# Weight conversion in a Strassen-style matmul kernel: three DVE passes put side by side, and GpSimd's addition made one instruction

## The chip, the cores and the metric

The kernel runs on one core of one Trainium2 chip. The metric is the device time of one execution in microseconds (us), lower is better. Each kernel was run several times, on the same chip in turn with the kernel before. Engines: PE is TensorE, DVE is VectorE, ACT is ScalarE, POOL is GpSimd.

## The reference

A cross attention between `x` and `state` gives 4352 rows of 512 numbers; they go through two weight matrices with a cosine gate between:

```python
h = x @ w_in              # (4352, 512) @ (512, 2048)
g = h * np.cos(h)
return (g @ w_out).astype(np.float32)
```

The matrices come as float64 (`randn(...).astype(float32)` times a NumPy float64 scalar), and the kernel turns both into float32 itself, from the raw 32-bit words.

## The kernel before

The program is one list of instructions for each engine, written in steps; a step makes one 128x512 tile of `h`, gates it, and lets TensorE multiply the gated tile of three steps ago with `w_out`. Steps 0 to 15 (about 30 to 130 us) also convert the weights, one load of 128x1024 elements a step. A load passes through three engines:

```python
if p == "1":   nc.scalar.activation(dst, raw_high_word, func=ACTF.Abs)
elif p == "2": nc.scalar.activation(e, raw_low_word, func=ACTF.Copy, scale=2.0 ** -51, bias=2.0)
elif p == "a": nc.vector.tensor_scalar(dst, dst, 2.0 ** -15, None, op0=ALU.max)          # limit
elif p == "b": nc.vector.tensor_scalar(bits, bits, 3, None, op0=ALU.logical_shift_left)  # shift
elif p == "c": nc.vector.scalar_tensor_tensor(out=bits, in0=raw_high, scalar=-2 ** 31, in1=bits,
                                              op0=ALU.bitwise_and, op1=ALU.bitwise_xor)  # sign
else:                                                                                    # d, the sum
    n = 1 if i < 4 else 2
    for j in range(n):
        r = slice(m * j // n, m * j // n + m // n)
        nc.gpsimd.tensor_tensor(bits[:, r], bits[:, r], e.bitcast(I32)[:, r], op=ALU.add)
```

(The views of the raw words are shortened here.) The loop over steps, cut to what matters:

```python
hidden(t)                          # PE: the tile h
go(0)                              # PE: attention and column-block products of this step
gate(t); gate2(t)                  # ACT: round; DVE: distance
go(1); go(3)                       # ACT and DVE: copies, attention
if last >= 0: convert(last, "cd")  # DVE c, POOL d of the load of the step before
gate3(t)                           # ACT: Abs, Sin
gate4(t)                           # DVE: gate product h * cos
...
if conv >= 0: convert(conv, "2")   # ACT, this step's load ("1" is further up)
go(4)
if conv >= 0: convert(conv, "ab")  # DVE
...                                # PE: output products of an earlier tile
```

So DVE's row in a step is gate2, c, gate4, a, b.

## Time and profile before

| | before |
|---|---|
| median of 6 runs | 821.08 us (820.25 to 821.51) |
| profiled span | 818.6 us |
| busy PE, DVE, ACT, POOL | 779.7, 435.0, 397.6, 184.0 us |
| PE idle from 30 to 135 us | 19.1 us |
| PE idle from 160 to 750 us | 4.2 us |

The busy shares of the whole run hide that there are two stages: up to about 130 us TensorE waits for the others, afterwards it is full. What is gained in the first stage moves the whole second stage forward. The lines for this are in the prediction.

### The profile page before, as it was taken

To read this page: it belongs to the slowest core of one execution; us is meant where nothing else is said; L and a number is where in the kernel's file an instruction comes from. 1 tells how busy PE (TensorE), PEld (TensorE's weight loads), DVE (VectorE), ACT (ScalarE), POOL (GpSimd) and SP (SyncE) were. 2 spreads that over 40 slices of the span, in tenths; PEclk is the share of its full clock that TensorE was granted. 3 is DMA by queue.
4 is the path that set the end of the run, shared out by engine and by line. 5 is a ranking of instruction groups with operands and counts; after the bars stand their busy time and mean duration, and the time that the engine had idled before them with its cause. 6 is when DMAs were issued, how large, how long until landed. Compare 5 with 4: busy or idle time off the path is not lost.

```text
span 818.6 us, 7603 instructions
## 1 busy us (share of the span) xinstructions
PE 779.7 (95%) x2736; PEld 349.9 (43%) x2736; DVE 435.0 (53%) x671; ACT 397.6 (49%) x644; POOL 184.0 (22%) x135
## 2 busy tenths in 40 slices
PE   6788788989999999999999999999999999999997
PEld 3233234334434443444444344444344444455554
DVE  3899897653355435863454456743554355432431
ACT  2667775554447444644455444634473445322222
POOL 2244237876100000154000000451000002620200
PEclk7899999999999999999999999999999999999999
DMA  6575350101000211030010211120000112100021
GB/s 154 180 213 178 123 155 1 26 8 45 1 15 12 52 26 26 13 65 0 1 26 7 58 23 16 33 46 0 14 14 0 27 26 54 75 1 13 14 38 38
DMA packets 111653, 37.19 MB, mean 45 GB/s; under 512 B 103616, under 2 KB 103616, under 8 KB 111616
## 3 DMA queue, kind: packets, MB, share of 16 engines
q1 hardware_dynamic: 108800, 35.93, 18.1%
q10 hardware_dynamic: 2688, 0.66, 0.4%
q8 instruction: 21, 0.34, 0.2%
q0 software_dynamic: 128, 0.13, 0.1%
q14 instruction: 16, 0.13, 0.1%
HBM read 27.79 MB, written 8.91 MB: 45 GB/s over the span
## 4 chain that ended last, share of the span: by engine, by line
PE 78%; DVE 11%; ACT 7%; issue 1%; DMA 1%; POOL 0%; ACTq 0%; DVEq 0%; POOLq 0%
PE o L504 42%; PE h L439 25%; PE at L291 4%; PE o L621 3%; DVE q L448 2%; PE at L378 2%; ACT q L454 1%; PE at L264 1%; DVE g_all L460 1%; ACT q L453 1%; DVE xT L311 1%; DVE aT L355 1%; ACT xT L337 1%; DVE w_in L226 1%; DVE w_in L221 1%
## 5 line engine op out<-in xcount | busy, mean ns | idle before, releaser
L439 PE MATMUL h<-aT,sw 128*128 128x512 f32 x512 | 247.8, 607 | 16.4 <-DVE g_all L460 11.9
L504 PE MATMUL o<-g_all,w_out 128*128 128x512 f32 x512 | 238.7, 603 | 4.5 <-DVE sw L418 2.9
L466 POOL TENSOR_TENSOR g_all<-g_all 128x512 f32<-128x512 f32 x80 | 112.0, 1421 | 460.7 <-DVE g_all L460 455.7
L445 ACT ACTIVATE q<-h 128x512 f32<-128x512 f32 (+1 forms) x144 | 82.2, 571 | 270.2 <-PE h L439 270.2
L448 DVE SCALAR_TENSOR_TENSOR q<-q,h 128x512 f32<-128x512 f32 (+1 forms) x144 | 94.2, 654 | 208.8 <-ACT q L445 208.8
L504 PE MATMUL o<-g_all,s 128*128 128x512 f32 x384 | 177.3, 598 | 0.0
L460 DVE TENSOR_TENSOR g_all<-h,q 128x512 f32<-128x512 f32 (+1 forms) x144 | 94.8, 658 | 139.5 <-ACT q L454 139.3
L439 PEld LDWEIGHTS h<-aT,sw 128*128 128x128 f32 x512 | 98.0, 194 | 145.5 <-issue 112.1
L504 PEld LDWEIGHTS o<-g_all,w_out 128*128 128x128 f32 x512 | 93.9, 190 | 127.1 <-issue 120.6
L453 ACT ACTIVATE q<-q 128x512 f32<-128x512 f32 (+1 forms) x144 | 87.5, 608 | 103.7 <-DVE q L448 103.7
L504 PEld LDWEIGHTS o<-g_all,s 128*128 128x128 f32 x384 | 70.3, 190 | 88.4 <-issue 83.6
L454 ACT ACTIVATE q<-q,halfpi 128x512 f32<-128x512 f32 (+1 forms) x144 | 100.5, 698 | 4.5
L236 POOL TENSOR_TENSOR w_out<-w_out,s 128x512 int32<-128x512 int32 x20 | 27.2, 1379 | 84.8 <-DVE w_out L226 80.0
L466 DVE TENSOR_TENSOR g_all<-g_all 128x512 f32<-128x512 f32 x48 | 33.2, 692 | 1.6
L439 PE MATMUL h<-sT,w_in 128*128 128x256 f32 x128 | 30.2, 379 | 0.0
L236 POOL TENSOR_TENSOR w_in<-w_in,s 128x512 int32<-128x512 int32 x16 | 21.7, 1369 | 37.7 <-DVE w_in L226 37.7
L420 ACT COPY sw<-at 128x512 f32<-128x512 f32 x48 | 25.7, 588 | 9.0 <-PE at L291 9.0
L621 PE MATMUL o<-w_out,g_all 128*128 128x512 f32 x64 | 29.6, 592 | 0.0
L439 PEld LDWEIGHTS h<-sT,w_in 128*128 128x128 f32 x128 | 24.3, 190 | 10.1 <-issue 6.7
L510 DVE SCALAR_TENSOR_TENSOR held<-o,held 128x512 f32<-128x512 f32 x40 | 25.4, 681 | 3.7 <-PE o L504 3.7
L291 PE MATMUL at<-w_in,stT 64*32 64x512 f32 x384 | 26.1, 601 | 0.0
L531 DVE STREAM_TRANSPOSE ot<-held 128x512 f32<-128x512 f32 x32 | 22.2, 694 | 0.0
(84 smaller groups left out, 472.5 us busy)
## 6 DMA issues: line engine op xcount, KB each, us to landing
out_dram<-ot SPq DMA_DIRECT2D x136, 64.0 KB, 2.0
g_all<-in_moe_w_out_dram SPq DMA_DIRECT2D x8, 1024.0 KB, 5.0
x_b<-in_x_dram SPq DMA_DIRECT2D x60, 128.0 KB, 2.9
g_all<-in_moe_w_in_dram SPq DMA_DIRECT2D x6, 1024.0 KB, 5.2
g_all<-in_moe_w_in_dram SPq DMA_DIRECT2D x4, 512.0 KB, 5.6
x_b<-in_moe_w_out_dram SPq DMA_DIRECT2D x1, 1024.0 KB, 5.7
xT<-in_moe_w_out_dram SPq DMA_DIRECT2D x1, 1024.0 KB, 7.8
x_b<-in_x_dram ACTq DMA_DIRECT2D x4, 128.0 KB, 4.7
```

The source lines that it names most:

```text
L236: nc.gpsimd.tensor_tensor(bits[:, r], bits[:, r], e.bitcast(I32)[:, r], op=ALU.add)
L291: nc.tensor.matmul(out=(to or at)[j][Ns * k:Ns * k + Ns, 0:n], lhsT=w[D * j:D * j + D, self.b, Ns * k:Ns * k + Ns], rhs=r(slice(D * j, D * ...
L420: nc.scalar.copy(dst, to[j][:, 0:c1 - c0])
L439: nc.tensor.matmul(out=t.hp, lhsT=t.lhs(i), rhs=t.rhs(i), start=(i == 0), stop=(i == t.kn - 1))
L445: nc.scalar.activation(t.q, t.hp, func=ACTF.Copy, bias=MAGIC)
L448: nc.vector.scalar_tensor_tensor(out=t.q, in0=t.q, scalar=MAGIC, in1=t.hp, op0=ALU.subtract, op1=ALU.subtract)
L453: nc.scalar.activation(t.q, t.q, func=ACTF.Abs)
L454: nc.scalar.activation(t.q, t.q, func=ACTF.Sin, bias=halfpi, scale=-TWO_PI)
L460: nc.vector.tensor_tensor(t.g, t.hp, t.q, op=ALU.mult)
L466: engine.tensor_tensor(out, a, b, op=ALU.subtract)
L504: nc.tensor.matmul(out=acc[bank][ch], lhsT=w[:, i, P * ch:P * ch + P], rhs=g.g, start=(i == 0), stop=(i == NH - 1))
L621: nc.tensor.matmul(out=acc[MAIN][i], lhsT=t.g[:, P * i:P * i + P], rhs=w_out[:, :, t.f, :], start=(n == 0), stop=(n == NF - 1))
```

## The change

The intent: limit and shift leave the end of a step, where GpSimd's sum of the load before is running and blocks them (limit takes 1.32 and shift 1.64 us there, 54.76 to 57.75 us, against 0.68 and 0.69 us with GpSimd idle, at 753.9 us), and stand beside the sign, in the time that ACT takes from distance to gate product. GpSimd's sum becomes one instruction in place of two halves. The whole diff (blank lines left out):

```diff
-            n = 1 if i < 4 else 2
-            for j in range(n):
-                r = slice(m * j // n, m * j // n + m // n)
-                nc.gpsimd.tensor_tensor(bits[:, r], bits[:, r],
-                                        e.bitcast(I32)[:, r], op=ALU.add)
+            nc.gpsimd.tensor_tensor(bits, bits, e.bitcast(I32), op=ALU.add)
@@ before step 0
     a0.exp2()
-    convert(3, "ab")
@@ in the step, between gate2 and gate4
         if last >= 0:
-            convert(last, "cd")
+            convert(last, "abcd")
@@ at the end of the step
         go(4)
-        if conv >= 0:
-            convert(conv, "ab")
```

## The prediction

> **What bounds the kernel now.** I read the 40 slices first, then the busy times by stretch, then the chain of waits from 30 to 130 us, and last the instructions of VectorE (DVE) and GpSimd (POOL) there in order of time.
>
> ```profile
> PE   6788788989999999999999999999999999999997
> PEld 3233234334434443444444344444344444455554
> DVE  3899897653355435863454456743554355432431
> ```
>
> One slice is 20.5 us. From the eighth slice TensorE is full to the end; only the first six (to about 130 us) leave it idle, and there DVE is at 80 to 90%. By stretch (start:end, length, then busy time and count of PE, weight loads, DVE, ACT, POOL; granted clock, DMA share, GB/s):
>
> ```profile
> 30.00:60.00 30.00, 24.24 (x112) 10.46 (x111) 25.35 (x37) 21.59 (x32) 10.87 (x9) 0.89 0.70 211
> 60.00:90.00 30.00, 26.16 (x104) 10.63 (x103) 28.43 (x36) 20.15 (x28) 13.25 (x10) 0.94 0.52 176
> 90.00:110.00 20.00, 14.65 (x61) 5.74 (x61) 16.05 (x22) 15.35 (x23) 5.44 (x4) 0.91 0.30 104
> 110.00:135.00 25.00, 20.88 (x78) 8.38 (x75) 21.28 (x28) 17.38 (x26) 13.37 (x10) 0.93 0.30 86
> 160.00:750.00 590.00, 585.77 (x2038) 259.32 (x2037) 289.05 (x460) 281.52 (x464) 107.32 (x75) 1.00 0.12 24
> ```
>
> Between 30 and 135 us TensorE's idle is 5.76 + 3.84 + 5.35 + 4.12 = 19 us of 105; from 160 to 750 us it is 4 of 590. So the change can only earn in these 105 us, and at most 19 us, 2.3% of 821. These are the sixteen first tiles (steps 0 to 15), during which the weights are turned into float32, one load a step. The chain of waits goes here through DVE and ACT. Two steps of DVE, in order of time (start, duration, line):
>
> ```profile
> 52.89 1.23 DVE L226 SCALAR_TENSOR_TENSOR w_out<-g_all,w_out 128x1024 int32<-128x1024 int32 x1
> 54.15 0.69 DVE L460 TENSOR_TENSOR g_all<-h,q 128x512 f32<-128x512 f32 x1
> 54.76 1.32 DVE L221 TENSOR_SCALAR w_in<-w_in 128x1024 f32<-128x1024 f32 x1
> 56.11 1.64 DVE L223 TENSOR_SCALAR w_in<-w_in 128x1024 int32<-128x1024 int32 x1
> 57.67 0.67 DVE L448 SCALAR_TENSOR_TENSOR q<-q,h 128x512 f32<-128x512 f32 x1
> 58.27 1.21 DVE L226 SCALAR_TENSOR_TENSOR w_in<-g_all,w_in 128x1024 int32<-128x1024 int32 x1
> ```
> POOL in the same time:
> ```profile
> 54.26 2.93 POOL L236 TENSOR_TENSOR w_out<-w_out,s 128x512 int32<-128x512 int32 x2 [5.39 <-DVE w_out L226]
> ```
>
> I call limit a (L221), shift b (L223), sign c (L226), POOL's sum d (L236), distance gate2 (L448), gate product gate4 (L460). Pool's d starts as c ends; a and b, behind gate4, run into it. Alone a takes 0.68 and b 0.69 us (as at 753.9 us, where POOL is idle); here they take 1.32 and 1.64. The two halves of d, 1.26 us each alone, take 2.93 instead of 2.5. Over the steps I add up what a, b and one small tensor-scalar of the attention take beyond 0.68, 0.69 and 0.20: 14.2 us of blocked DVE.
>
> [...]b waits out POOL's second half and ends 0.56 us after it (57.75 against 57.19)[...]. [...]the two block sums of 1024 elements on POOL show 2.35 us, and the instruction behind one starts 2.32 us after it (132.06 to 134.38), so I use 2.35.
>
> **The change part by part.** No instruction of PE, DVE or ACT goes or comes. In steps 0 to 15 DVE's order gate2, copies and attention, c, gate4, attention, a, b becomes gate2, copies and attention, a, b, c, gate4, attention: a and b of a load leave the end of the step of its scalar passes and stand before its c in the next one. On POOL 28 halves of d (loads 4 to 17) become 14 whole ones, and 4 late halves 2.
>
> *What it removes.* In a bare step of before, gate4 0.6, a 1.3, b 1.65, gate2 0.67, then Abs 0.64 and Sin 0.72 on ACT, which nothing of DVE but c covers: 5.5 to 5.8 us from c to c (c at 52.89, 58.27, 63.75). After, the loop is the lock: c 1.2, d 2.4 with its start, a 0.56 behind the release, b 0.72: 4.9 to 5.0 us. gate4 and gate2 fall under d, Abs and Sin under a, b, c. So a bare step gains 0.5 to 0.8 us. d whole saves POOL 2.9 - 2.35 = 0.55 us[...].
>
> *What it adds.* Where a and b stood in the shade, they now stand in the path. Step 1: POOL is idle, ACT still busy, so a and b (1.4 us) delay gate4; minus 0.4 that gate2 comes sooner: about +1.0. Step 3: the products of the second column block wait for d of load 5; before, a and b of load 6 ran in that wait, after they follow the copies and the keeping of the reads: about +0.9, with TensorE's first output product 2.0 us later behind the whole d.
>
> *The sum.* I went through DVE, ACT and POOL step by step with the durations of before and these orders. End of gate4 against before: step 1 +1.0, step 3 +0.9, 4 +0.2, 5 -0.2, 6 -0.6, 7 -0.5, 8 -0.2 (7 and 8 are full of DVE work of the attention, their a and b were hardly blocked), 9 -1.2 (gate2 comes 2.3 earlier, and the exponentials on ACT with it), 10 -2.2, 11 -1.9, 12 -2.8, 13 -4.2, 14 -4.0, 15 -4.8 us. Of the 14.2 us of blocking only a third comes out, because a now waits for the whole d instead (about 1 us in a bare step) and ACT's own row, gate 0.5, Abs 0.64, Sin 0.72, two scalar passes 2 x 1.05 and copies 0.5 to 1.1, is 4.5 to 5.1 us.
>
> Behind step 16 TensorE is full and everything shifts alike; of the 19 us of idle 14 remain. The two late loads (750 to 775 us) have steps of 6.87 us in which DVE idles some 3 to 5; a and b there delay gate4 by about 1.4 us with no one waiting: nothing. Ideal walk-throughs lose something to waits that I did not see, so I take 4.1 us: 821.1 - 4.1 = 817.0 us.
>
> **The rivals.** *The lock disappears altogether.* If a met a POOL that had finished, 14 us would come back, 807 us. For it: a and b lie 1.3 us later after c than before. Against it: gate4 and gate2 are only 1.3 us, d is 2.35. It needs copies or attention between, as in steps 7 and 10. *The late consumer.* Two halves let the first rows be used early; whole d and later c could stall TensorE at steps 3 and 4 by 2 us and never give it back, if ACT is the bound after: 821 to 823 us. For it: TensorE waits for POOL at L291 and L504 now, 6.0 and 5.5 us at its weight loads. Against it: only one products call comes within a step of its load, and DVE was longer than ACT in all four stretches. *The loads.* A raw slot is freed by c; if steps shorten, ACT's first pass may wait for the DMA. A load takes 5 to 8 us (5.2 us median), and my walk leaves 1 to 7 us between landing and use except for the last load, which comes about 1 us late under cover: costs at most 1 to 2 us, 818 to 819 us.
>
> **Range and chances.** 812.5 to 820.5 us: the lower end is the walk plus some 4 us of the blocking that I still count, the upper is a gain all but eaten by steps 1, 3 and 4. A gain of 2% (16.4 us) would need 86% of TensorE's idle time; a loss of 2% would need every step 1 us longer. Faster by over 2%: 0.03, within: 0.94, slower: 0.03.
>
> **What would show it.** Right: b at 0.69 us everywhere, a between 1.0 and 1.9 us in bare steps, d at 2.35 us, c to c near 5.0 us, the first output product of TensorE near 57.6 us instead of 55.58, gate4 of step 15 near 125 instead of 129.76 us, idle of TensorE from 30 to 130 us less by 4 to 5. Wrong: a not blocked (the first rival), or c to c over 5.4 us with DVE waiting for ACT, or idle at TensorE behind step 16.

The walk came to 4.8 us at step 15, I took 4.1, 821.1 - 4.1 = 817.0 us. What is called the lock, or blocked, is what the trace before shows beside POOL's sum: limit at 1.32 and shift at 1.64 us, in place of 0.68 and 0.69, and shift ending 0.56 us after the sum's second half. That a and b would be held in the same way behind a whole sum was my estimate.

## The result, and the profile after

The changed kernel takes 819.81 us (median of 6 runs, 817.97 to 820.05) against 821.08. The ratio is 0.998, 95% interval 0.9967 to 0.9993. The class "within 2%" was right, the range held it, but of the 4.1 us that I forecast 1.3 came.

The slices of the changed kernel, with the clock that TensorE was granted:

```profile
PE   6659789989999999999999999999999999999997
DVE  3777896663364435863464446743554355432531
PEclk8989999999999999999999999999999999999999
```

The third slice (41 to 61 us) shows PE at 5 tenths where before it had 8: a new hole. By stretch, columns as in the prediction:

```profile
30.00:60.00 30.00, 18.03 (x96) 7.89 (x95) 21.23 (x34) 22.21 (x32) 8.46 (x5) 0.90 0.65 196
60.00:90.00 30.00, 27.05 (x99) 12.00 (x98) 24.58 (x35) 19.53 (x27) 11.36 (x5) 0.96 0.48 158
90.00:110.00 20.00, 16.43 (x68) 5.58 (x68) 17.37 (x24) 17.90 (x26) 5.16 (x3) 0.93 0.37 137
110.00:135.00 25.00, 22.07 (x88) 9.77 (x89) 21.35 (x29) 16.04 (x25) 12.99 (x6) 0.93 0.34 96
160.00:750.00 590.00, 585.76 (x2041) 259.66 (x2040) 289.17 (x460) 280.57 (x463) 106.23 (x75) 1.00 0.12 24
```

DVE has less to do, as intended (428.9 instead of 435.0 us over the run, POOL 178.3 instead of 184.0). But TensorE's idle from 30 to 60 us doubles, from 5.8 to 12.0 us. Over 30 to 135 us it is 11.97 + 2.95 + 3.57 + 2.93 = 21.4 us, more than the 19.1 of before, not 4 to 5 less.

The same loads on DVE and POOL as in the prediction (c of load 6 to c of load 7), changed kernel:

```profile
55.16 1.23 DVE L226 SCALAR_TENSOR_TENSOR w_out<-g_all,w_out 128x1024 int32<-128x1024 int32 x1
56.42 0.69 DVE L454 TENSOR_TENSOR g_all<-h,q 128x512 f32<-128x512 f32 x1
57.03 0.68 DVE L442 SCALAR_TENSOR_TENSOR q<-q,h 128x512 f32<-128x512 f32 x1
57.62 1.81 DVE L221 TENSOR_SCALAR w_in<-w_in 128x1024 f32<-128x1024 f32 x1
59.46 0.69 DVE L223 TENSOR_SCALAR w_in<-w_in 128x1024 int32<-128x1024 int32 x1
60.19 1.23 DVE L226 SCALAR_TENSOR_TENSOR w_in<-g_all,w_in 128x1024 int32<-128x1024 int32 x1
...
56.53 2.35 POOL L231 TENSOR_TENSOR w_out<-w_out,s 128x1024 int32<-128x1024 int32 x1 [7.75 <-DVE w_out L226]
```

This is the loop that was forecast: limit (L221) waits out the sum and ends 0.55 us after it (59.43 against 58.88), shift (L223) is free at 0.69, and from c to c it is 5.03 us instead of 5.38. The loss must lie elsewhere. TensorE's long waits, first in the kernel before, with the one before its first output product (55.58 us), then in the changed one (in the brackets: idle time just before, and who ended it):

```profile
55.58 1.98 PE L504 MATMUL o<-g_all,w_out 128*128 128x512 f32 x4 [1.61 <-POOL w_out L236]
66.79 0.66 PE L264 MATMUL at<-ident,x_b 128*128 128x128 f32 x4 [2.76 <-ACT xT L273]
96.96 2.56 PE L504 MATMUL o<-g_all,w_out 128*128 128x512 f32 x4 [2.90 <-DVE sw L418]
124.86 3.22 PE L439 MATMUL h<-aT,sw 128*128 128x512 f32 x4 [2.69 <-DVE g_all L460]
```

```profile
48.84 1.93 PE L285 MATMUL o<-w_in,stT 64*32 64x512 f32 x8 [3.98 <-POOL w_in L231]
58.94 3.61 PE L498 MATMUL o<-g_all,w_out 128*128 128x512 f32 x4 [4.07 <-POOL w_out L231]
88.60 2.87 PE L433 MATMUL h<-aT,sw 128*128 128x512 f32 x4 [2.95 <-DVE g_all L454]
123.91 3.55 PE L433 MATMUL h<-aT,sw 128*128 128x512 f32 x4 [2.93 <-DVE g_all L454]
```

The first output product comes 3.4 us later than before, and then its four matmuls take 3.61 us in place of 1.98. The granted clock (third number from the end) tells why; before, then after:

```profile
48.00:52.00 4.00, 3.36 (x25) 1.59 (x24) 3.85 (x8) 2.54 (x4) 0.87 (x1) 1.00 0.68 245
60.00:64.00 4.00, 4.00 (x14) 1.82 (x12) 3.60 (x5) 2.98 (x5) 2.67 (x2) 1.00 0.79 261
124.00:128.00 4.00, 3.13 (x5) 1.12 (x5) 3.94 (x5) 0.18 (x1) 2.93 (x2) 0.68 0.00 0
```

```profile
48.00:52.00 4.00, 3.17 (x20) 1.50 (x22) 1.18 (x2) 1.92 (x3) 0.78 (x1) 0.57 0.78 271
60.00:64.00 4.00, 4.00 (x8) 1.68 (x7) 1.98 (x3) 1.21 (x2) 2.35 (x1) 0.72 0.58 182
124.00:128.00 4.00, 4.00 (x20) 1.50 (x21) 3.93 (x4) 1.85 (x4) 1.63 (x1) 0.61 0.00 0
```

After each wait shown of 2.69 us or more TensorE works at a mean granted clock of 0.51 to 0.68 in the next 3.4 us; after the 1.61 us of the kernel before it keeps 1.00. In windows of 0.1 us the clock at each of these seven places is 0.50 for 3.41 us, then 1.00 again. This half clock begins from 0.24 us before (48.60 us) to 1.21 us after (98.17 us) the start of the first matmul behind the wait. The prediction has nothing of it. The kernel before loses its clock too, but elsewhere (0.57 from 40 to 44, 0.64 from 68 to 72, 0.68 from 124 to 128 us); from 30 to 135 us the mean granted clock is 0.92 before and 0.93 after. So the changed kernel does not have more low clock in all; it has it in steps 3 and 4, where the kernel before has none.

To see where the lead is won and lost, I use the start of gate4 in each step, changed kernel minus before (minus is earlier), next to the ledger of the prediction:

| step | forecast | changed kernel |
|---|---|---|
| 1 | +1.0 | +0.84 |
| 3 | +0.9 | +2.27 |
| 5 | -0.2 | +2.86 |
| 9 | -1.2 | +1.57 |
| 12 | -2.8 | -0.12 |
| 15 | -4.8 | -1.67 |
| 20 | -4.8 | -1.01 |

From step 5 to step 15 the changed kernel gains 4.53 us where 4.6 were forecast. That the sum fits to 0.1 us is partly luck: from step 12 to 15 only 1.55 of 2.0 us came, from 5 to 9 there were 1.29 instead of 1.0. It loses 3.1 us more than forecast up to step 5, and 0.7 us between 15 and 20. From step 20 to the last step (143) the lead is 1.0 us, except in steps 134 and 136 with the late loads (below). The two profiled spans differ by 0.5 us only (818.6 and 818.1): half of the lead goes between the last step and the end, and no run asks why.

### The profile page after: what moved, and what is told of

It is laid out like the page before. It is cut to its first block, busy times and chain, and to the rows that moved or that the text cites. A ratio compares the mean times of both kernels' runs of the same rounds, so it can differ in the third digit from the quotient of the medians.

```text
span 818.1 us, 7589 instructions
## 1 busy us (share of the span) xinstructions
PE 776.4 (95%) x2736; PEld 349.6 (43%) x2736; DVE 428.9 (52%) x671; ACT 397.9 (49%) x644; POOL 178.3 (22%) x119
## 4 chain that ended last, share of the span: by engine, by line
PE 79%; DVE 10%; ACT 7%; DMA 1%; POOL 1%; issue 1%; ACTq 0%; DVEq 0%; POOLq 0%
PE o L498 43%; PE h L433 25%; PE at L285 4%; PE o L615 3%; PE at L372 2%; DVE q L442 2%; PE at L258 1%; ACT q L448 1%; DVE xT L305 1%; DVE g_all L454 1%; ACT q L447 1%; DVE aT L349 1%; ACT q L439 1%; ACT xT L331 1%; DVE w_in L226 1%; DMA x_b<-in_x_dram 1%
## 5 line engine op out<-in xcount | busy, mean ns | idle before, releaser
L231 POOL TENSOR_TENSOR w_out<-w_out,s 128x1024 int32<-128x1024 int32 x10 | 23.9, 2390 | 86.3 <-DVE w_out L226 83.6
L231 POOL TENSOR_TENSOR w_in<-w_in,s 128x1024 int32<-128x1024 int32 (+1 forms) x10 | 19.3, 1931 | 42.0 <-DVE w_in L226 39.3
```

What stands on the lines that cost most here:

```text
L231: nc.gpsimd.tensor_tensor(bits, bits, e.bitcast(I32), op=ALU.add)
```

## The experiments

Theory A: the gain of the moved passes is there; it is lost to TensorE's waits for whole sums in steps 3 to 5 and at the handover to its full stretch (steps 14 to 17), and above all to the half clock (0.50) after those waits. Rival B: moved passes lose by themselves, whole sums are innocent. Rivals C and D: whatever is won in the steps is lost again where TensorE becomes the bound. Ten kernels ran, all with correct results, five rounds each (4 to 6 timed runs). They ran on three chips (e1 to e4, e6 to e9, e10 and e11), each beside the kernel before, so times of different groups are compared by their ratios.

| kernel | median us | before us | ratio (95% interval) |
|---|---|---|---|
| e1_move_only | 815.21 | 820.27 | 0.9939 (0.9927 to 0.9951) |
| e2_pool_one | 820.64 | 820.27 | 1.0008 (0.9996 to 1.002) |
| e3_fill | 818.47 | 820.27 | 0.9972 (0.9958 to 0.9986) |
| e4_shade | 814.59 | 820.27 | 0.9925 (0.9912 to 0.9938) |
| e6_fill16 | 818.41 | 820.58 | 0.9973 (0.9957 to 0.999) |
| e7_fill_all | 816.07 | 820.58 | 0.995 (0.9939 to 0.9962) |
| e8_shade_fill | 813.88 | 820.58 | 0.9916 (0.9903 to 0.9929) |
| e9_before_fill16 | 820.35 | 820.58 | 0.9996 (0.9984 to 1.0008) |
| e10_half15 | 817.19 | 820.31 | 0.9957 (0.9942 to 0.9973) |
| e11_shade_whole | 815.34 | 820.31 | 0.9937 (0.9925 to 0.9949) |

Start of gate4 against before, in us, in the profiled run of each. How far single profiles scatter can be read from programs that are alike up to a step: e6 and e10 are the changed kernel up to step 12 and repeat its +2.86 at step 5 with +2.87 and +2.78, but e9 is the kernel before up to step 15 and stands at +0.91 there. Step 0 itself lies between -0.61 (e11) and +0.10 (e8). So differences of up to some 0.9 us in this table show nothing by themselves.

| step | e1 | e2 | e3 | e4 | e6 | e7 | e8 | e9 | e10 | e11 |
|---|---|---|---|---|---|---|---|---|---|---|
| 1 | +0.83 | -0.18 | +0.72 | -0.02 | +0.66 | +0.92 | +0.10 | -0.16 | +0.93 | -0.61 |
| 3 | +2.50 | +0.01 | +1.30 | +1.42 | +2.21 | +1.48 | +0.68 | +0.71 | +2.36 | +0.57 |
| 5 | +2.08 | +0.89 | +0.26 | +0.28 | +2.87 | +0.44 | -0.46 | +0.91 | +2.78 | -0.47 |
| 12 | -0.92 | +0.65 | -2.75 | -2.89 | -0.07 | -2.46 | -4.30 | +0.90 | -0.24 | -3.50 |
| 15 | -3.56 | +0.52 | -4.32 | -5.52 | -1.61 | -4.02 | -6.92 | +0.70 | -2.87 | -5.06 |
| 20 | -4.31 | -0.23 | -2.31 | -6.27 | -2.36 | -4.77 | -7.67 | -0.04 | -3.63 | -5.81 |

### e1_move_only: one part of the change alone

```diff
# against the changed kernel
-            nc.gpsimd.tensor_tensor(bits, bits, e.bitcast(I32), op=ALU.add)
+            n = 1 if i < 4 else 2
+            for j in range(n): ...   # as in the kernel before
```

> The changed kernel with POOL's sum in two halves again, the move of limit and shift alone. Theory A (the loss sits in steps 3 to 5, where TensorE waits for a whole sum, idles 4 us twice and then runs at half clock): with halves the first consumers start 1.1 us earlier, [...]the clock stays at 1.00, gate4 of step 5 comes at 66 us or before (68.13 in the changed kernel), and the bare steps stay near 5.0 us, because two halves and a whole cost limit and shift the same end (3.7 us after the sign). Time 817 to 818.5 us. Rival B (the moved limit and shift themselves lose in steps 1 and 3, the whole sum is innocent): step 5 stays at 67.5 to 68.5 us, and the bare steps get worse as limit collides with the second half: 820 to 822 us.

Measured: 0.9939, 5 us faster than before and better than either theory had it. Moving the passes is good by itself, so in the time rival B falls; the whole sum takes back two thirds of the gain (0.2% is left of 0.61%). But step 5 comes at 67.35 us, not at 66, close to the 67.5 of rival B, after waits of 2.91 and 3.07 us with a clock of 0.57 from 48 to 52 and 0.75 from 60 to 64 us: a missed expectation. The halves bring at most 0.8 us there, less than the scatter. The larger part comes later. In step 14 a tensor-scalar of two columns stands behind the sum of load 15; first the changed kernel, then this one:

```profile
117.51 1.43 DVE L341 TENSOR_SCALAR i<-i 128x2 f32<-128x2 f32 x1
```

```profile
116.92 0.28 DVE L345 TENSOR_SCALAR i<-i 128x2 f32<-128x2 f32 x1
```

It waits 1.2 us longer for a whole sum. And the full stretch begins at full clock here (1.00 from 120 to 132 us), so the lead grows from 3.56 to 4.31 us at step 20, instead of shrinking. In the bare steps (those in which DVE has next to no copies or attention) the whole sum is worth nothing: from step 9 to 13 the two kernels gain the same, 2.98 us with whole sums (+1.57 to -1.41), 3.10 with halves (+1.04 to -2.06).

### e2_pool_one: the other part alone

```diff
# against the kernel before
-            n = 1 if i < 4 else 2
-            for j in range(n): ...
+            nc.gpsimd.tensor_tensor(bits, bits, e.bitcast(I32), op=ALU.add)
```

> The kernel before with POOL's sum in one, nothing moved. Theory A: the late consumers of steps 3 and 4 wait for a whole sum, while limit and shift still run into it; 0.2 us a step lost in bare steps, and the first output product goes from 55.6 to 57 us or later[...]: 821.5 to 824 us. Rival B: the whole sum only saves POOL 0.55 us a load: 819.5 to 821 us.

Measured: 1.0008, no difference, below what theory A expected and within the range of rival B. The first output product did slide, less than expected, and ran at half clock (0.50 from 56 to 60 us):

```profile
56.66 3.78 PE L499 MATMUL o<-g_all,w_out 128*128 128x512 f32 x4 [2.69 <-POOL w_out L232]
```

It is 0.89 us behind at step 5, no more than e9 is without any whole sum. It won 0.7 us back at the handover, where the profiled run of the kernel before had its clock at 0.68 and this one at 1.00. The 0.2 us a step that I expected in bare steps did not appear.

### e3_fill: keep TensorE busy in steps 3 and 4

```diff
# against the changed kernel
+    def fill(n):        # results unused; the bank is overwritten afterwards
+        for _ in range(n):
+            nc.tensor.matmul(out=acc[0][0], lhsT=w_in[:, 0, 0:P],
+                             rhs=w_in[:, 0, 0:WC], start=True, stop=True)
@@ column-block products of step 3, between the k that are there and those that wait
+                if between and k == 1: fill(between)      # 4
@@ end of step 4, before the first output product
+        if step == 4: fill(4)
```

> The changed kernel with eight matmuls that nobody uses, four in TensorE's wait in step 3 and four in its wait in step 4, to a free bank that is overwritten afterwards; results stay right. Only the clock can change by it. Theory A: the clock stays at 1.00 from 44 to 63 us, the eight products of step 3 take 1.1 us instead of 1.93 and the first output product 2.0 instead of 3.61; gate4 of step 5 comes 1.5 to 2.5 us earlier than 68.13, the steady lead over the kernel before grows from 1.0 to 2 to 3 us: 817.5 to 819 us. Rival C (what is won is lost again where TensorE becomes the bound, at steps 15 to 17): step 5 gains but the lead at step 20 stays at 1.0 us, 819.5 to 820.5 us.

Measured: 0.9972. Step 5 comes at 65.53 instead of 68.13 us, and the ledger down to step 15 is close to the forecast (-4.32 against -4.8). Only the clock can have brought this, which stays at 1.00 from 44 to 64 us: the sum of load 5, on which step 3 waits, ends at 48.68 us against 48.78, and the eight products behind it take 1.06 us instead of 1.93. Then 2 us of the lead disappear before step 20, and the clock shows where:

```profile
120.00:124.00 4.00, 2.73 (x4) 1.18 (x5) 3.93 (x5) 1.35 (x2) 2.35 (x1) 0.57 0.00 0
124.00:128.00 4.00, 4.00 (x21) 1.08 (x20) 3.44 (x6) 1.98 (x4) 2.33 (x2) 0.57 0.00 0
```

The six runs fall into two groups, 815.75 and 815.93 at a mean clock of 0.991 and 0.986, and 818.42 to 819.22 at 0.982 to 0.983.

### e4_shade: limit and shift of three loads at their old place, halves

```diff
# against e1_move_only
+    SHADE = {3, 4, 6}      # and convert(3, "ab") before step 0 again
-            convert(last, "abcd")
+            convert(last, "cd" if last in SHADE else "abcd")
         go(4)
+        if conv in SHADE:
+            convert(conv, "ab")
```

> Halves as before, and limit and shift of loads 3, 4 and 6 at their old place (behind the step of their scalar passes), of the others at the new one. Theory A with my ledger: step 1 no longer +0.8, step 3 no longer +2.3 but about 0, step 5 about -0.3, and the later steps earn the same 4.5 us from step 5 to 15: lead of 3 to 4.5 us at step 15, 816.5 to 818 us. Rival C: lead at step 20 of 1 to 1.5 us whatever step 5 does: 819.5 to 820.5 us.

Measured: 0.9925, faster than expected: -5.52 at step 15 and -6.27 at step 20. Step 3 is +1.42, not the 0 expected, with the clock still at 0.57 from 48 to 52 us; but the first output product waits 1.61 us only and runs in 1.99. This version beats the kernel before by 5.7 us on the medians (820.27 - 814.59), and its interval lies clear of the changed kernel's.

### e6_fill16 and e7_fill_all: the handover

```diff
# against the changed kernel; fill as in e3_fill, with the bank as an argument
+        if step in FILLS: fill(*FILLS[step])      # e6: {16: (3, 0)}
         hidden(t)                                 # e7: {10: (3, 1), 16: (3, 0)} and the fills of e3
```

> The changed kernel with three unused matmuls at the start of step 16 alone, where TensorE waits 2.9 us for gate4 of step 14 and then starts its full stretch at half clock (0.61 from 124 to 128 us). Theory A (part of the lead is lost at the handover by the half clock): clock 1.00 there, steps 0 to 15 unchanged (gate4 of step 15 about 1.7 us ahead of the kernel before), the lead at step 17 grows instead of shrinking: about 2.4 us instead of 1.0, ratio 0.997. Rival D (the lead shrinks from step 15 to 17 because TensorE has a backlog): the fills only lengthen the backlog, lead 1.0 us or less, ratio 0.998 to 0.999.

> The changed kernel, its order of DVE and its whole sums untouched, with unused matmuls in all four long waits of TensorE (steps 3, 4, 10 and 16). Theory A: with the clock at 1.00 throughout, the ledger of the prediction holds: gate4 of step 5 within 0.5 us of the kernel before, of step 15 4 to 5 us ahead, and this time kept to the end: ratio 0.994 to 0.995, about 815.5 us. Rival D: 4 us ahead at step 15, 2.3 or less at step 20, ratio 0.997 as with the fills of steps 3 and 4 alone.

Measured: 0.9973 and 0.995. In e6 nothing changes up to step 15 (-1.61), and then the lead grows to 2.36 instead of shrinking to 1.01. In e7, which has the changed kernel's DVE and POOL rows to the letter, the lead is 4.02 us at step 15 and 4.77 at step 20. The forecast was 4.8 at both; that 4.77 meets it is luck, as 0.75 of it is the low clock of the kernel before at its own handover (0.68). The clock of e7:

```profile
60.00:64.00 4.00, 4.00 (x17) 2.28 (x16) 2.68 (x5) 2.27 (x5) 2.35 (x1) 1.00 0.64 192
124.00:128.00 4.00, 4.00 (x24) 1.48 (x9) 3.97 (x6) 1.26 (x4) 2.03 (x1) 1.00 0.00 0
```

The interval of e7 lies clear of the changed kernel's (0.9967 to 0.9993); that of e6 overlaps it, and there the trace decides. Rivals C and D fall: what is won before step 16 stays, if TensorE enters its full stretch at full clock. The kernel before with fills in all its waits was not run; so it is open how much of the 4.77 us such fills would have won without the reorder.

### e9_before_fill16: a control on the kernel before

```diff
# against the kernel before
+        if step in FILLS: fill(*FILLS[step])      # {16: (3, 0)}
         hidden(t)
```

> Control: the kernel before with three unused matmuls at the start of step 16, where its TensorE waits 2.7 us and then runs at a clock of 0.68 from 124 to 128 us. Theory A: clock 1.00 there, step 17 comes 0.7 to 1.4 us earlier, ratio 0.9983 to 0.9992. Rival D: no gain, 1.000.

Measured: 0.9996, inconclusive in time. In the trace the handover works as expected (+0.70 at step 15 to -0.04 at step 20). But this profiled run had lost 0.9 us by step 5 with a clock of 0.62 from 48 to 52 us, where the profiled run of the kernel before had 1.00, although the two programs are alike up to step 16. And it loses 0.45 us more at step 29 (+0.41 from there to the end). So the clock is not decided by the program alone; a single profile may not be read as if it were.

### e10_half15 and e11_shade_whole: which sums, which places

```diff
# e10 against the changed kernel: the old loop, with
+            n = 2 if i == 15 else 1
# e11 against the changed kernel: SHADE of e4_shade, whole sums
```

> The changed kernel with POOL's sum of load 15 alone in two halves. In the changed kernel the small tensor-scalar of step 14 waits 1.2 us for that whole sum, in e1_move_only it does not. Theory A: it drops from 1.43 to 0.3 us, gate4 of step 14 and 15 come 0.9 to 1.1 us earlier (lead at 15 about 2.7 instead of 1.7 us), TensorE's wait at step 16 shrinks from 2.9 to about 2 us and the full stretch need not start at half clock: lead at step 20 of 2 to 3.4 us, ratio 0.996 to 0.9975. Rival D: the lead at step 20 stays at 1.0, ratio 0.998.

> The changed kernel, whole sums, with limit and shift of loads 3, 4 and 6 at their old place: tells the place of the three loads from the halves in e4_shade. If the place alone is what costs up to step 5, gate4 of step 5 comes as in e4_shade, 65.3 to 66 us, and the end differs from it only by the whole sum of load 15 and the handover (lead 3 to 4.5 us at step 15, 2 to 3 at step 20, ratio 0.9965). If the whole sums of loads 5 and 6 cost as well, TensorE's waits in steps 3 and 4 stay near 4 us, the clock falls there, and step 5 comes at 66.5 to 67.5 us: ratio 0.997 to 0.998.

Measured: 0.9957 and 0.9937, both better than expected; the interval of e10 still touches the changed kernel's (0.9973 and 0.9967). In the profiles, one halved sum out of sixteen moves the lead at step 20 from 1.01 to 3.63 us: the small tensor-scalar takes 0.34 us, and TensorE waits 1.84 us at step 16 and keeps its clock (1.00 from 124 to 128 us):

```profile
122.71 1.98 PE L437 MATMUL h<-aT,sw 128*128 128x512 f32 x4 [1.84 <-DVE g_all L458]
```

In e11 the place of three loads alone brings step 5 from +2.86 to -0.47, although TensorE still waits 4 us in step 3; what is gone is the 4 us wait before the first output product:

```profile
48.33 1.93 PE L285 MATMUL o<-w_in,stT 64*32 64x512 f32 x8 [4.05 <-POOL w_in L231]
57.24 1.98 PE L498 MATMUL o<-g_all,w_out 128*128 128x512 f32 x4 [1.83 <-POOL w_out L231]
```

So up to step 5 it is the place of limit and shift of loads 3, 4 and 6 that costs, 3.3 us here (-0.47 against +2.86), 2.9 if counted from step 0. What the whole sums cost there is not shown: 0.78 us by e1 (+2.08 against +2.86) and 0.89 by e2, but -0.75 by e4 and e11 (+0.28 with halves, -0.47 with whole sums), all within the scatter that e9 shows.

### e8_shade_fill: e4 with fills

```diff
# against e4_shade: 3 fills in step 3, and
+    FILLS = {10: (3, 1), 16: (2, 0)}
```

> Halves, limit and shift of loads 3, 4 and 6 at their old place, and fills in the waits of steps 3, 10 and 16. Theory A: the runs of e4_shade fall in two groups, 812 and 814.6 us, which I take for a clock that is low or not at one of the waits; with fills all runs are in the lower group: 811.5 to 813 us, ratio 0.990 to 0.991, lead 6.5 us or more at step 20. If the two groups have another cause, the median stays at 814 to 814.6.

Measured: 0.9916. The lead in the profile, which is that of the fastest run, is 7.67 us as expected, but the runs are 812.73 to 814.32, median 813.88, not 811.5 to 813. Against e4 (0.9925) the intervals overlap. The fills may help by 0.7 us or not at all; what spreads these runs over 1.6 us is open.

## Why the prediction was right or wrong

**The bound, the lock, the bare steps: right.** Only the first 130 us could earn, and the lead is constant afterwards. (The slices were read too kindly: the ninth of the kernel before is at 8, with a wait of 1.86 us before 169.7 us, which is 1.86 us in the changed kernel too.) Limit runs at 1.2 to 1.95 us where it meets the sum, shift at 0.69 to 0.70, the sum in 2.35, c to c 5.03 us (105.07 to 110.12: 5.05) against the forecast of 4.9 to 5.0. The 5.5 to 5.8 us of before were a sum of parts; the three starts of c that stand beside it give 5.38 and 5.48. From step 5 to 15 the gain is 4.53 us of 4.6.

**"What it adds", step 3: the term that failed.** I put step 3 at +0.9 us and the first output product 2.0 us later. They came at +2.27 and 3.4 us, and step 5 at +2.86 instead of -0.2. I had taken TensorE's instructions at the durations of the kernel before, which at this place are those of full clock. Behind the longer waits (3.98 and 4.07 us) the clock was 0.50 for 3.41 us each time: 1.93 us for eight matmuls, 3.61 for the four of the first product, and the hidden tile behind it reached ACT at 64.30 us; 57.6 us and the 3.7 us that the product and this tile take in the kernel before would have given 61.3. Keeping TensorE busy there, without touching the order on DVE and POOL, brings step 5 to +0.26 (e3) and +0.44 (e7): 2.4 to 2.6 of the 3.06 us that were missing are the clock. The rest lies in step 3, which even with fills comes at +1.30 (e3) and +1.48 (e7) against +0.9: limit and shift of load 6 stand in the path there with 1.4 us (53.71 to 55.12 us, neither blocked).

**"Behind step 16 TensorE is full and everything shifts alike": wrong at the joint.** It holds from step 17 on. Between 15 and 17 the changed kernel loses 0.67 us because TensorE, after 2.93 us of idle, starts its stretch at 0.61; with fills it gains 0.75 (e6). That is 1.4 us (the 0.75 are a low clock of the kernel before that the changed one then no longer has). Together with the first term, 2.6 + 1.4 = 4.0 us, against a difference of 3.8 between e7 and the changed kernel at step 20 (4.77 - 1.01).

**The rival "the late consumer" was set aside too fast.** It named the right place and a bound of 2 us for the loss, and I gave it only that bound. What makes it larger is not the wait itself but the clock behind it. Of the two causes that it names, "whole d and later c", the runs show the later c, that is the moved limit and shift of loads 3, 4 and 6 (3.3 us by e11). The share of the whole d up to step 5, on which my theory A had put the loss, cannot be told from the scatter (e1, e2, and e4 with e11).

**The whole sum: forecast as a small gain, measured as a loss.** The 0.55 us that it saves POOL earned nothing in bare steps (e1 against the changed kernel, 3.10 against 2.98 us), since two halves with limit between them cost nearly the same: from c to c 4.90 us in e1 (120.16 to 125.06) and 5.04 in the changed kernel (121.91 to 126.95). It costs where a short instruction waits for it: 1.2 us at step 14, which through the handover became 2.6 us (e10). The prediction names neither that wait nor what TensorE makes of it.

**The other rivals.** The lock did not disappear, but this rival, and with it a sign that I had named for being wrong, came half true: of the 14 loads of 1024 elements in the first 130 us limit waits in five only (1.21 to 1.95 us) and takes 0.65 to 0.74 us in the nine others, where the sum was over when it came. The 14.2 us of blocking fall to 6.9 in the trace of the changed kernel; what came out did not shorten the path by as much. ACT's first pass over a load (L214) sat idle for no transfer in the changed kernel. The two late loads delay gate4 of steps 134 and 136 by 1.45 us against the lead, and TensorE keeps its 1.0 us, as forecast.

## What to carry to other kernels

When a walk through a trace makes an engine wait longer, the work behind the wait need not keep its duration on TensorE (here 3.61 us for four matmuls in place of 1.98): reckon with a low clock behind it, or fill the wait with matmuls that nobody reads (e7: clock 1.00 at the four places, ratio 0.995 in place of 0.998). All 21 waits of 2.69 us or more, between 30 and 133 us in the profiles of the kernel before, the changed one, e1 to e4, e10 and e11, have a stretch of 4 us at a mean clock of 0.50 to 0.77 at or behind them. Of the shorter waits some do and some do not: after 2.07 us (at 106.3 us) e1 was granted 0.54 up to 110.0 us, after 2.15 us (at 38.97 us) the kernel before 0.67 over the next 3.4 us; after 2.55 us (at 35.83 us) and 2.07 us (at 106.95 us) the changed kernel kept 1.00. Programs that are alike do not always get the same: e3 is the changed kernel up to step 3, and behind the same wait (2.54 us, at 35.74 us) its eight products took 1.08 us, against 0.64 us in the changed kernel; its runs lie at 815.8 and at 818.4 to 819.2 us, the faster at the higher mean clock (0.986 to 0.991 against 0.982 to 0.983). What decides it was not tested. The waits are those between matmul records, whose ends the profile models.

Merging two instructions of the engine that others wait for won nothing here (e2: 1.0008); look first for the short instructions that wait for it: a tensor-scalar of 128x2 elements took 1.43 us behind a whole sum and 0.28 us behind a half, and one halved sum of GpSimd was worth 2.6 us of lead in the profiles (e10).
